# Float64 weights to float32: the integer add of the conversion moves from GpSimd to VectorE

## The chip, the core and the metric

The kernel runs on one core of a Trainium2 chip. The metric is the device time of one launch in microseconds. Before the change it is 1539.69 us, the median of 3 runs (1537.06 to 1542.2); a profile of one execution goes with them.

## What is computed

Attention over queries pooled in pairs, then two MLPs (pairs of dense layers) one behind the other:

```
q_pool = q.reshape(B, H, S // 2, 2, D).mean(axis=3)          # B=4, H=8, S=1152, D=64
scores = (q_pool @ k^T) / sqrt(D);  attn = softmax(scores);  x = attn @ v
x: (2304, 512) tokens
h = x @ w_in;  g = max(0.01 * h, h);              x = g @ w_out      # first MLP, d_ff = 2048
h = x @ w_in2; g = where(h > 0, h, exp(h) - 1);   out = g @ w_out2   # second MLP
```

The weights of both MLPs arrive as float64 (a 128x512 piece is 512 KB), everything else as float32. The products are wanted in nearly full float32 precision: each float32 operand is split into a high part and a low part, and three matmuls (high x high, high x low, low x high) stand for one.

## The kernel before

The work is written down as a list of small operations, each with an engine, a guessed cost, a rank and the buffers that it reads and writes (`Program.add`, L57). `Program.schedule` (L83) plays the list through once with the guessed costs: when an engine is free it takes the ready operation of lowest rank. The start times that come out of it set the order in which instructions are issued, and on the chip each engine then works through its own queue strictly in that order. An operation may issue several instructions; they stand together in the queue.

The attention of four batches (16 pairs of heads) and eight MLP passes (four batches, two layers) overlap: while the attention of one batch runs, the MLP of an earlier batch is worked in between (`PLAN`, L216). TensorE does scores (L452), transposes (L475), attention x v (L496), the first matmul of an MLP (L638) and the second one (L676). VectorE takes row maxima of scores (L457, L459), low parts of the attention weights (L267, `pt`), parts of the activation functions (L651, L659) and sums of partial products (L689). ScalarE does the exponentials (L463) and high parts (L261). GpSimd does the low parts of weights and activations: the line L267 with `wi`, `wo`, `g`, `kn`, `vn`, `qn`.

A weight piece is used in four batches. The first time it comes as float64 and is converted by `convert` (L271), half of it at a time: 128 halves of 128x256 numbers in all. The float32 result is kept in DRAM (L328), and the three later uses load it from there (L323). The conversion of one half is this:

- SyncE loads the half as pairs of 32-bit words into `cr` (L290): `r[:, :, 0]` low words, `r[:, :, 1]` high words. There are two `cr` buffers, so a load waits until the last reader of the half but one is done.
- VectorE shifts the high word left by 3 and masks it (L293), then puts the two top bits back (L296). The result is `ct`.
- ScalarE scales the low word down to the three bits that are still wanted, in place (L299), and takes the magnitude of the high word, read as a float, into `cm` (L301).
- GpSimd adds the three bits to `ct` as an integer (L303).
- VectorE sets values too small to be represented to zero and writes the piece `wr` (L305). ScalarE and GpSimd then split `wr` into `wi` or `wo` (L331 and L333, through `psplit`, L258).

`cr` is free for the next load when L299, L301, L293, L296 and L303 have read it.

Of the kernel before, what the change touches and what calls it, by code (L numbers as in the profile page):

```python
# [9 lines left out]
F32 = mybir.dt.float32  # L10
F32R = mybir.dt.float32r
U32 = mybir.dt.uint32
ACTF = mybir.ActivationFunctionType
ALU = mybir.AluOpType
# [140 lines left out]
def kernel(  # L155
# [20 lines left out]
    V, A, G, PE = nc.vector, nc.scalar, nc.gpsimd, nc.tensor  # L176
# [10 lines left out]
    FT = DFF // 128  # L187
    QSCALE = 0.5 / float(D) ** 0.5
    HB = NQ // 2
    MIN_HI = 2.0 ** (112 - 127) * (1 + 2.0 ** -3)  # L190
    PTB = 4
    CW = 256
    CB = 2
# [47 lines left out]
    prog = Program()  # L241

    def sb(tag, shape, dt=F32, bufs=1):
        return prog.buf(tag, bufs, lambda: sp.tile(shape, dt, tag=tag, name=tag, bufs=bufs))
# [4 lines left out]
    def act(n, accum=False, sbuf=False):  # L249
        return 50 + 0.833 * n + (190 if accum else 0) + (43 if sbuf else 0)  # L250

    def dve(n, fast=False):
        return 66 + (0.52 if fast else 1.05) * n

    def pool(n):
        return 140 + 2.12 * n
# [14 lines left out]
    def convert(rank, dst, src):  # L271

        for n in range(0, 512, CW):
            r = sb("cr", [128, CW, 2], U32, CB)
            t = sb("ct", [128, CW], U32, CB)  # L280
            mag = sb("cm", [128, CW], F32, CB)

            def load(n=n, r=r):
                rv = r.ap.rearrange("p n t -> p (n t)")
                if len(src.shape) == 3:
                    k0, kn = n // src.shape[2], CW // src.shape[2]
                    rv, sv = rv.rearrange("p (c n) -> p c n", c=kn), src[:, k0:k0 + kn, :]
                else:
                    sv = src[:, n:n + CW]
                nc.sync.dma_start(out=rv, in_=sv.bitcast(U32))  # L290

            prog.add("SP", 60, rank - 1, load, w=[r])
            prog.add("DVE", dve(CW, True), rank, lambda r=r, t=t: V.tensor_scalar(  # L293
                out=t.ap, in0=r[:, :, 1], scalar1=3, scalar2=0x3FFFFFF8,
                op0=ALU.logical_shift_left, op1=ALU.bitwise_and), w=[t], r=[(r, 1)])
            prog.add("DVE", dve(CW), rank, lambda r=r, t=t: V.scalar_tensor_tensor(  # L296
                out=t.ap, in0=r[:, :, 1], scalar=0xC0000000, in1=t.ap,
                op0=ALU.bitwise_and, op1=ALU.bitwise_or), w=[t], r=[(r, 1), t])
            prog.add("ACT", act(CW, sbuf=True), rank, lambda r=r: A.activation(  # L299
                out=r[:, :, 0], in_=r[:, :, 0], func=ACTF.Copy, scale=2.0 ** -29), w=[(r, 0)], r=[(r, 0)])  # L300
            prog.add("ACT", act(CW, sbuf=True), rank, lambda r=r, mag=mag: A.activation(  # L301
                out=mag.ap, in_=r[:, :, 1].bitcast(F32), func=ACTF.Abs), w=[mag], r=[(r, 1)])
            prog.add("POOL", pool(CW), rank, lambda t=t, r=r: G.tensor_tensor(  # L303
                out=t.ap, in0=t.ap, in1=r[:, :, 0], op=ALU.add), w=[t], r=[t, (r, 0)])
            prog.add("DVE", dve(CW), rank, lambda n=n, t=t, mag=mag: V.scalar_tensor_tensor(  # L305
                out=dst[:, n:n + CW], in0=mag.ap, scalar=MIN_HI, in1=t.ap.bitcast(F32),
                op0=ALU.is_ge, op1=ALU.mult), w=[(dst, n)], r=[t, mag])

    kept = {}

    def load_w(rank, layer, w_in, w_out, f, mine):

        src = (w_in[:, f * 128:(f + 1) * 128].rearrange("(c p) f -> p c f", p=128),
               w_out[f * 128:(f + 1) * 128, :])
        rs = [mine("wr", [128, 512], F32, WRB, "p", PBUF) for _ in range(2)]
        for i, r in enumerate(rs):
            if w_in.dtype == F32:
                view = (lambda r=r: r.ap.rearrange("p (c n) -> p c n", c=DC)) if i == 0 else lambda r=r: r.ap
                prog.add("SP", 60, rank - 1.5, lambda i=i, view=view: nc.sync.dma_start(
                    out=view(), in_=src[i]), w=[r])  # L320
            elif (layer, f, i) in kept:
                kp = kept[layer, f, i]
                prog.add("SP", 60, rank - 1.5, lambda r=r, kp=kp: nc.sync.dma_start(  # L323
                    out=r.ap, in_=kp.ap), w=[r], r=[kp])
            else:
                convert(rank - CLEAD, r, src[i])
                kp = kept[layer, f, i] = Buf(lambda i=i: dram.tile([128, 512], F32, name=f"w{layer}_{f}_{i}"))
                prog.add("SP", 60, rank, lambda r=r, kp=kp: nc.sync.dma_start(out=kp.ap, in_=r.ap), w=[kp], r=[r])  # L328
        wi = mine("wi", [128, 2, DC, 128], F32R, WIB, "qT", KTB)
        wo = mine("wo", [128, 2, DM], F32R, WOB, "kT", KTB)  # L330
        psplit(rank - 0.5, WH, WL, lambda: wi[:, 0].rearrange("p c n -> p (c n)"),  # L331
               lambda: wi[:, 1].rearrange("p c n -> p (c n)"), lambda: rs[0].ap, 512, (wi, 0), [rs[0]])
        psplit(rank - 0.5, WH, WL, lambda: wo[:, 0], lambda: wo[:, 1], lambda: rs[1].ap, 512, (wo, 0), [rs[1]])  # L333
        return wi, wo
# [3 lines left out]
    for j in range(2):  # L338
        t = sp.tile([128, 2, 128], F32R, name=f"rem{j}")
# [400 lines left out]
    for b, layer, at, wide in PLAN:  # L740
        tags = [(u, size[u]) for u in ("h" * HBUFS + ("t" * TB + "s" * SBUFS if wide else ""))]
        w = ((moe_w_in, moe_w_out), (moe2_w_in, moe2_w_out))[layer]
# [35 lines left out]
```

## Time and profile before

| | |
|---|---|
| median of 3 runs | 1539.69 us |
| span of the profiled execution | 1538.0 us |
| TensorE matmul busy | 1414.5 us (92%) |
| VectorE busy | 1011.8 us (66%) |
| ScalarE busy | 1065.2 us (69%) |
| GpSimd busy | 829.8 us (54%) |
| granted TensorE clock, mean | 0.988 of 2.4 GHz |

The profiled execution's span, first to last instruction, is 1.7 us under the median of the timed runs. Busy shares over the whole span hide that it has stages. Conversions run in two stretches, up to some 80 us and from 200 to 590 us; in the latter VectorE is busy nearly all the time. After 590 us all weights are converted and TensorE is busy nearly all the time.

### The profile page before, as it was taken

The numbers are of one execution on the slowest core, as the hardware profiler recorded it, in microseconds if no ns is written. First come the engines' busy times: TensorE is split into PE (matmuls) and PEld (weight loads), VectorE is DVE, ScalarE is ACT, GpSimd is POOL, SyncE is SP. The second block draws the span as 40 slices with busy tenths as digits, with TensorE's granted clock in tenths as the row PEclk, the third lists the DMA queues.
The fourth block names the chain that finished last, engine by engine and source line by source line (L and its number), as shares of the span: only waits on it lengthen the run. The fifth ranks groups of instructions, "written<-read, shape, count | busy, mean of one in ns | idle before, by whom it ended". The sixth has DMA issues, their size and how long they took to land.

```text
span 1538.0 us, 28928 instructions
## 1 busy us (share of the span) xinstructions
PE 1414.5 (92%) x10288; PEld 1365.5 (89%) x10288; DVE 1011.8 (66%) x2273; ACT 1065.2 (69%) x2901; POOL 829.8 (54%) x840
## 2 busy tenths in 40 slices
PE   5877889988888898999999999999999999999998
PEld 4777788888778887999999999899999998899998
DVE  6999888899998998556665556556665454123222
ACT  6998878776688787676668777676667773443553
POOL 5443355765766667354555555255555445466661
PEclk9999999999999999999999999999999999999999
DMA  4232123344434443222222222222222222323210
GB/s 147 91 115 87 40 77 121 122 130 129 127 119 139 132 143 118 76 75 69 69 68 86 79 78 64 71 71 61 76 71 64 56 63 63 106 77 89 70 55 32
DMA packets 82642, 135.59 MB, mean 88 GB/s; under 512 B 8512, under 2 KB 26944, under 8 KB 82496
## 3 DMA queue, kind: packets, MB, share of 16 engines
q1 hardware_dynamic: 82496, 133.73, 28.5%
q8 instruction: 81, 1.33, 0.4%
q14 instruction: 65, 0.53, 0.1%
HBM read 112.20 MB, written 21.50 MB: 87 GB/s over the span
## 4 chain that ended last, share of the span: by engine, by line
PE 63%; DVE 20%; ACT 7%; DMA 4%; issue 3%; POOL 2%; SPq 0%; ACTq 0%; POOLq 0%; DVEq 0%
PE h L676 16%; PE h L638 16%; PE s L452 8%; PE o L496 7%; PE t L475 5%; DVE m L457 3%; DVE ct L293 3%; DVE wr L305 3%; PE s L638 3%; PE s L676 3%; DVE ct L296 2%; DVE pt L267 2%; PE t L638 2%; PE t L373 2%; PE t L676 2%
## 5 line engine op out<-in xcount | busy, mean ns | idle before, releaser
L676 PE MATMUL h<-g,wo 128*128 128x288 f32 x2460 | 425.8, 303 | 16.7 <-DVE t L659 7.9
L638 PE MATMUL h<-xs,wi 128*128 128x288 f32 x2448 | 418.1, 305 | 23.3 <-DVE t L659 13.5
L638 PEld LDWEIGHTS h<-xs,wi 128*128 128x128 f32 x2448 | 351.8, 190 | 33.1 <-DVE t L659 19.0
L676 PEld LDWEIGHTS h<-g,wo 128*128 128x128 f32 x2460 | 356.9, 189 | 23.1 <-DVE t L659 9.9
L457 DVE TENSOR_REDUCE m<-s 128x1 f32<-128x384 f32 x432 | 231.8, 550 | 71.9 <-PE s L452 68.9
L261 ACT ACTIVATE pt<-t 128x384 fp32r<-128x384 f32 (+2 forms) x426 | 188.0, 456 | 117.3 <-PE t L475 109.1
L463 ACT ACTIVATE p<-s,m 128x384 f32<-128x384 f32 x432 | 249.1, 587 | 19.1 <-DVE m L459 18.7
L267 DVE TENSOR_TENSOR pt<-t,pt 128x384 fp32r<-128x384 f32 (+1 forms) x416 | 206.6, 508 | 74.0 <-ACT pt L261 72.6
L452 PE MATMUL s<-kT,qT 128*128 128x384 f32 x768 | 198.5, 356 | 25.7 <-ACT p L463 25.0
L267 POOL TENSOR_TENSOR g<-t,g 128x288 fp32r<-128x288 f32 x216 | 179.1, 833 | 67.6 <-ACT g L261 62.4
L267 POOL TENSOR_TENSOR wo<-wr,wo 128x512 fp32r<-128x512 f32 x112 | 145.9, 1307 | 108.2 <-ACT wo L261 106.3
L496 PE MATMUL o<-pt,vn 128*128 128x256 f32 (+1 forms) x1152 | 192.1, 302 | 5.4 <-DVE pt L267 3.5
L475 PE MATMUL t<-ident,p 128*128 128x128 f32 x1116 | 181.8, 277 | 12.3 <-DVE pt L267 11.3
L267 POOL TENSOR_TENSOR wi<-wr,wi 128x512 fp32r<-128x512 f32 x110 | 144.0, 1310 | 62.9 <-ACT wi L261 48.9
L496 PEld LDWEIGHTS o<-pt,vn 128*128 128x128 f32 x1152 | 165.1, 190 | 10.4 <-DVE pt L267 10.0
L475 PEld LDWEIGHTS t<-ident,p 128*128 128x128 f32 x1116 | 139.8, 142 | 21.9 <-DVE pt L267 11.8
L452 PEld LDWEIGHTS s<-kT,qT 128*128 128x128 f32 x768 | 126.2, 193 | 32.9 <-ACT p L463 31.8
L303 POOL TENSOR_TENSOR ct<-ct,cr 128x256 uint32<-128x256 uint32 x128 | 98.8, 774 | 95.5 <-DVE ct L296 33.8
L267 POOL TENSOR_TENSOR vn<-raw,vn 128x576 fp32r<-128x576 f32 x32 | 46.3, 1448 | 174.5 <-ACT vn L261 174.5
L261 ACT ACTIVATE g<-t 128x288 fp32r<-128x288 f32 x216 | 95.9, 446 | 44.1 <-DVE t L659 26.2
L689 DVE TENSOR_TENSOR acc<-h,acc 128x288 f32<-128x288 f32 x158 | 71.0, 452 | 66.2 <-PE h L676 64.9
L261 ACT ACTIVATE wo<-wr 128x512 fp32r<-128x512 f32 x112 | 70.5, 630 | 46.3 <-PE h L676 33.5
(150 smaller groups left out, 2228.4 us busy)
## 6 DMA issues: line engine op xcount, KB each, us to landing
wr<-w SPq DMA_DIRECT2D x172, 256.0 KB, 2.7
cr<-in_moe_w_in_dram SPq DMA_DIRECT2D x64, 256.0 KB, 2.8
cr<-in_moe_w_out_dram SPq DMA_DIRECT2D x64, 256.0 KB, 2.7
w<-wr SPq DMA_DIRECT2D x64, 256.0 KB, 2.4
raw<-in_k_dram SPq DMA_DIRECT2D x32, 288.0 KB, 3.0
raw<-in_v_dram SPq DMA_DIRECT2D x32, 288.0 KB, 3.1
raw<-in_q_dram SPq DMA_DIRECT2D x32, 256.0 KB, 2.9
p<-w SPq DMA_DIRECT2D x20, 256.0 KB, 2.6
```

The costliest lines, as they stand in the source:

```text
L261: prog.add("ACT", act(n, sbuf=not psum), rank, lambda: A.activation(out=hi(), in_=src(), func=ACTF.Copy), w=[w], r=r)
L267: lambda: eng.tensor_tensor(out=lo(), in0=src(), in1=f32(hi()), op=ALU.subtract),
L293: prog.add("DVE", dve(CW, True), rank, lambda r=r, t=t: V.tensor_scalar(out=t.ap, in0=r[:, :, 1], scalar1=3, scalar2=0x3FFFFFF8, op0=ALU.l ...
L303: prog.add("POOL", pool(CW), rank, lambda t=t, r=r: G.tensor_tensor(out=t.ap, in0=t.ap, in1=r[:, :, 0], op=ALU.add), w=[t], r=[t, (r, 0)])
L452: PE.matmul(out=st[:, 0:384], lhsT=qa(a), rhs=kT[:, 384 * c:384 * c + 384], start=(i == 0), stop=(i == len(seq) - 1))
L457: prog.add("DVE", dve(384), rank - LR, lambda st=st, c=c: V.tensor_reduce(out=m[:, c:c + 1], in_=st[:, 0:384], axis=AX.X, op=ALU.max), w=[ ...
L463: prog.add("ACT", act(384, True), rank - LE, lambda c=c: A.activation(out=p[:, 384 * c:384 * c + 384], in_=banks[c][:, 0:384], func=ACTF.E ...
L475: PE.transpose(out=t[:, i, :], in_=p[:, (3 * c + i) * 128:(3 * c + i + 1) * 128], identity=ident)
L496: PE.matmul(out=o[:, 0:n], lhsT=vn[:, c, :], rhs=pt[th][:, a, c % 3, :], start=(c == 3 * ORDER[0] and a == 0), stop=(c == 3 * ORDER[2] + 2 ...
L638: PE.matmul(out=h[:, 0:HB], lhsT=wi[:, a, c, :], rhs=xs[c][:, e, cols], start=(c == 0 and a == 0 and e == 0), stop=(c == DC - 1 and a == 1))
L676: PE.matmul(out=y[:, 0:HB], lhsT=w[f][1][:, a, d * 128:(d + 1) * 128], rhs=g[f][:, e, cols], start=(f % FC == 0 and a == 0 and e == 0), st ...
L689: prog.add("DVE", dve(HB), rank - HURRY, lambda y=y, a_=a_, cols=cols: V.tensor_tensor(out=a_[:, cols], in0=y[:, 0:HB], in1=a_[:, cols], o ...
```

## The change

The conversion of a half keeps its load, its two ScalarE instructions and three VectorE instructions, and loses the GpSimd instruction. ScalarE multiplies the high word, read as a float, by 2^-112 (this moves its exponent to where float32 has it; values too small become zero) into `g`, which keeps the tag `cm`. VectorE then shifts `g` left by 3, adds the low word's three bits as integers and puts the sign bit of `g` back, writing the piece. These three are one operation of the schedule, so they stand one behind the other in VectorE's queue, and each reads what the one ahead of it wrote. Lines behind the change have numbers lower by 3 in the changed kernel.

```
-            prog.add("DVE", dve(CW, True), rank, lambda r=r, t=t: V.tensor_scalar(
-                out=t.ap, in0=r[:, :, 1], scalar1=3, scalar2=0x3FFFFFF8,
-                op0=ALU.logical_shift_left, op1=ALU.bitwise_and), w=[t], r=[(r, 1)])
-            prog.add("DVE", dve(CW), rank, lambda r=r, t=t: V.scalar_tensor_tensor(
-                out=t.ap, in0=r[:, :, 1], scalar=0xC0000000, in1=t.ap,
-                op0=ALU.bitwise_and, op1=ALU.bitwise_or), w=[t], r=[(r, 1), t])
+            prog.add("ACT", act(CW, sbuf=True), rank, lambda r=r, g=g: A.activation(
+                out=g.ap, in_=r[:, :, 1].bitcast(F32), func=ACTF.Copy, scale=REBIAS), w=[g], r=[(r, 1)])
             prog.add("ACT", act(CW, sbuf=True), rank, lambda r=r: A.activation(
                 out=r[:, :, 0], in_=r[:, :, 0], func=ACTF.Copy, scale=2.0 ** -29), w=[(r, 0)], r=[(r, 0)])
-            prog.add("ACT", act(CW, sbuf=True), rank, lambda r=r, mag=mag: A.activation(
-                out=mag.ap, in_=r[:, :, 1].bitcast(F32), func=ACTF.Abs), w=[mag], r=[(r, 1)])
-            prog.add("POOL", pool(CW), rank, lambda t=t, r=r: G.tensor_tensor(
-                out=t.ap, in0=t.ap, in1=r[:, :, 0], op=ALU.add), w=[t], r=[t, (r, 0)])
-            prog.add("DVE", dve(CW), rank, lambda n=n, t=t, mag=mag: V.scalar_tensor_tensor(
-                out=dst[:, n:n + CW], in0=mag.ap, scalar=MIN_HI, in1=t.ap.bitcast(F32),
-                op0=ALU.is_ge, op1=ALU.mult), w=[(dst, n)], r=[t, mag])
+            def join(n=n, g=g, t=t, r=r):
+                V.tensor_scalar(out=t.ap, in0=g.ap.bitcast(U32), scalar1=3, scalar2=None, op0=ALU.logical_shift_left)
+                V.tensor_tensor(out=t.ap, in0=t.ap, in1=r[:, :, 0], op=ALU.add)
+                V.scalar_tensor_tensor(
+                    out=dst[:, n:n + CW].bitcast(U32), in0=g.ap.bitcast(U32), scalar=0x80000000, in1=t.ap,
+                    op0=ALU.bitwise_and, op1=ALU.bitwise_or)
+
+            prog.add("DVE", dve(CW, True) + 2 * dve(CW), rank, join, w=[t, (dst, n)], r=[g, (r, 0)])
```

How VectorE's queue changes is seen around one cast of `qn` in the middle of the second stretch. `ct` is the integer result, `wr` the finished piece, `m` a row maximum, `pt` attention weights, `xu` the attention output. Before:

```order
L457 TENSOR_REDUCE m_6430<-s_6412 128x1
L296 SCALAR_TENSOR_TENSOR ct_6417<-cr_6370,ct_6417 128x256
L305 SCALAR_TENSOR_TENSOR wr_6440<-cm_6415,ct_6404 128x256
L509 TENSOR_TENSOR xu_5681<-o_6362,tm_6450 64x320
L305 SCALAR_TENSOR_TENSOR wr_6440<-cm_6433,ct_6417 128x256
L263 CAST qn_6475<-qs_5738 128x512
L457 TENSOR_REDUCE m_6430<-s_6481 128x1
L293 TENSOR_SCALAR ct_6494<-cr_6442 128x256
L296 SCALAR_TENSOR_TENSOR ct_6494<-cr_6442,ct_6494 128x256
L293 TENSOR_SCALAR ct_6510<-cr_6464 128x256
```

The same place of VectorE's queue in the changed kernel, where the shift is L298, the add L299 and the sign L300 (the add is listed as an instruction of its own kind, over 512 elements instead of 256):

```order
L298 TENSOR_SCALAR ct_6519<-cm_6497 128x256
L299 ISA ct_6519<-cr_6448,ct_6519 128x512
L300 SCALAR_TENSOR_TENSOR wr_6474<-cm_6497,ct_6519 128x256
L456 TENSOR_REDUCE m_6458<-m_6458 128x1
L263 CAST qn_6535<-qs_5668 128x512
L298 TENSOR_SCALAR ct_6561<-cm_6545 128x256
L299 ISA ct_6561<-cr_6485,ct_6561 128x512
L300 SCALAR_TENSOR_TENSOR wr_6564<-cm_6545,ct_6561 128x256
L506 TENSOR_TENSOR xu_5815<-o_6414,tm_6566 64x320
```

Before, the three VectorE instructions of a half lie apart, with those of other halves or other work between them; now they are always neighbours, and the second and the third name the `ct` that the one ahead of them writes.

GpSimd's queue around the low part of the same `qn`, before (`ct` is the integer add, the others are low parts):

```order
L267 TENSOR_TENSOR wo_6380<-wr_6356,wo_6380 128x512
L303 TENSOR_TENSOR ct_6404<-ct_6404,cr_6352 128x256
L303 TENSOR_TENSOR ct_6417<-ct_6417,cr_6370 128x256
L267 TENSOR_TENSOR qn_6475<-qs_5738,qn_6475 128x512
L267 TENSOR_TENSOR wi_6479<-wr_6440,wi_6479 128x512
L303 TENSOR_TENSOR ct_6494<-ct_6494,cr_6442 128x256
L303 TENSOR_TENSOR ct_6510<-ct_6510,cr_6464 128x256
```

and in the changed kernel:

```order
L267 TENSOR_TENSOR wo_6523<-wr_6218,wo_6523 128x512
L267 TENSOR_TENSOR qn_6535<-qs_5668,qn_6535 128x512
L267 TENSOR_TENSOR wo_6555<-wr_6376,wo_6555 128x512
L267 TENSOR_TENSOR g_6609<-t1_6580,g_6609 128x288
L267 TENSOR_TENSOR wi_6643<-wr_6298,wi_6643 128x512
```

The 128 adds are gone from GpSimd's queue; all its other work stays. ScalarE keeps its two instructions for a half, now with `cm` ahead of `cr`. The same number of loads and stores is issued by SyncE.

## Rows read from the trace of the kernel before

**Rows 1.** Windows of the whole span: busy us of each engine by stage.
```profile
core 0: us, PE busy (x) PEld busy (x) DVE busy (x) ACT busy (x) POOL busy (x), PEclk, DMA share, GB/s
...
200.00:300.00 100.00, 91.45 (x650) 85.51 (x650) 86.46 (x196) 80.66 (x228) 61.72 (x64) 0.98 0.32 103
300.00:590.00 290.00, 252.06 (x1769) 235.19 (x1767) 276.46 (x580) 220.53 (x619) 188.53 (x200) 0.99 0.42 133
590.00:1538.00 948.00, 917.88 (x6834) 905.83 (x6834) 476.62 (x1083) 594.00 (x1571) 495.98 (x485) 0.99 0.24 71
```

**Rows 2.** Chain that ended last, 300 to 590 us: its shares by line.
```profile
by line: DVE wr L305 10.9%; DVE ct L293 10.6%; DVE ct L296 9.5%; issue 7.9%; DVE m L457 7.2%; DVE pt L267 5.7%; PE h L638 4.8%; DMA cr<-in_moe_w_out_dram 4.6%; DVE acc L689 3.1%; ACT p L463 2.9%; DMA cr<-in_moe_w_in_dram 2.7%; POOL ct L303 
```

**Rows 3.** VectorE's groups by line, whole span: busy, mean ns, idle before.
```profile
L305 DVE SCALAR_TENSOR_TENSOR wr<-cm,ct 128x256 f32<-128x256 f32 x128 | 83.6, 657 | 1.7 <-POOL ct L303 1.6
L296 DVE SCALAR_TENSOR_TENSOR ct<-cr,ct 128x256 uint32<-128x256 uint32 x128 | 80.5, 632 | 0.9
L293 DVE TENSOR_SCALAR ct<-cr 128x256 uint32<-128x256 uint32 x128 | 69.8, 549 | 11.1 <-DMA cr<-in_moe_w_in_dram 8.9 <-DMA cr<-in_moe_w_out_dram 2.1
L538 DVE TENSOR_TENSOR xu<-t,xu 128x512 f32<-128x512 f32 x12 | 8.3, 690 | 0.8 <-PE t L535 0.6
```

**Rows 4.** Tiles ct and qs: durations min/median/max in ns.
```profile
L293 DVE TENSOR_SCALAR ct<-cr x128: 272/294/1524, 7.8 to 587.7; 128x256 uint32<-128x256 uint32 x128
L296 DVE SCALAR_TENSOR_TENSOR ct<-cr,ct x128: 403/425/1659, 9.4 to 589.2; 128x256 uint32<-128x256 uint32 x128
L303 POOL TENSOR_TENSOR ct<-ct,cr x128: 729/747/1034, 11.9 to 589.7; 128x256 uint32<-128x256 uint32 x128
L305 DVE SCALAR_TENSOR_TENSOR wr<-cm,ct x128: 402/416/1678, 12.7 to 591.4; 128x256 f32<-128x256 f32 x128
L399 DVE TENSOR_SCALAR qs<-qs x32: 229/286/1494, 8.6 to 1141.4; 128x256 f32<-128x256 f32 x32
```

**Rows 5.** Timeline of VectorE, 451 to 459 us: start, us, instruction.
```profile
451.92 0.28 DVE L293 TENSOR_SCALAR ct<-cr 128x256 uint32<-128x256 uint32 x1
452.24 0.93 DVE L296 SCALAR_TENSOR_TENSOR ct<-cr,ct 128x256 uint32<-128x256 uint32 x1
453.56 0.54 DVE L457 TENSOR_REDUCE m<-s 128x1 f32<-128x384 f32 x1
454.02 1.68 DVE L305 SCALAR_TENSOR_TENSOR wr<-cm,ct 128x256 f32<-128x256 f32 x1
456.95 1.33 DVE L293 TENSOR_SCALAR ct<-cr 128x256 uint32<-128x256 uint32 x1
458.32 0.42 DVE L296 SCALAR_TENSOR_TENSOR ct<-cr,ct 128x256 uint32<-128x256 uint32 x1
```

**Rows 6.** Timeline of GpSimd in the same stretch.
```profile
452.13 0.75 POOL L303 TENSOR_TENSOR ct<-ct,cr 128x256 uint32<-128x256 uint32 x1 [0.41 <-DVE ct L296]
453.99 1.43 POOL L267 TENSOR_TENSOR vn<-raw,vn 128x576 fp32r<-128x576 f32 x1
456.83 1.30 POOL L267 TENSOR_TENSOR wo<-wr,wo 128x512 fp32r<-128x512 f32 x1 [1.42 <-ACT wo L261]
```

**Rows 7.** GpSimd's groups by line, 300 to 590 us.
```profile
L303 POOL TENSOR_TENSOR ct<-ct,cr 128x256 uint32<-128x256 uint32 x84 | 65.0, 775 | 56.4 <-DVE ct L296 16.7 <-issue 7.1 <-ACT cm L301 4.8
L267 POOL TENSOR_TENSOR g<-t,g 128x288 fp32r<-128x288 f32 x42 | 36.8, 875 | 15.3 <-ACT g L261 12.0 <-DVE ct L293 2.1 <-DVE ct L296 0.9
L267 POOL TENSOR_TENSOR wo<-wr,wo 128x512 fp32r<-128x512 f32 x21 | 28.2, 1343 | 11.4 <-ACT wo L261 10.1 <-DVE ct L293 1.0
L267 POOL TENSOR_TENSOR wi<-wr,wi 128x512 fp32r<-128x512 f32 x21 | 28.2, 1341 | 7.9 <-ACT wi L261 4.7 <-DVE qs L399 1.8 <-PE s L452 1.1
L267 POOL TENSOR_TENSOR kn<-raw,kn 128x576 fp32r<-128x576 f32 x6 | 8.9, 1489 | 2.9 <-ACT kn L261 2.9
```

**Rows 8.** ScalarE's groups by line, 300 to 590 us.
```profile
L299 ACT ACTIVATE cr<-cr 128x256 uint32<-128x256 uint32 x84 | 36.7, 437 | 11.2 <-DMA cr<-in_moe_w_out_dram 8.2 <-DMA cr<-in_moe_w_in_dram 1.4 <-POOL ct L303 0.9
L301 ACT ACTIVATE cm<-cr 128x256 f32<-128x256 f32 x84 | 36.0, 429 | 0.0
```

**Rows 9.** Waits of SyncE's queue, and of TensorE from 300 to 590 us.
```profile
SPq L290 <- POOL ct L303: 188.4, 115, 8.4
PE h L638 <- DVE t L659: 10.3, 11, 1.7
```

More of the change, by code (lines that the diff above doesn't have):

```diff
@@ L189 @@
     HB = NQ // 2
-    MIN_HI = 2.0 ** (112 - 127) * (1 + 2.0 ** -3)
+    REBIAS = 2.0 ** -112
     PTB = 4
@@ L280, in convert @@
             t = sb("ct", [128, CW], U32, CB)
-            mag = sb("cm", [128, CW], F32, CB)
+            g = sb("cm", [128, CW], F32, CB)
             def load(n=n, r=r):
```

## The prediction

> **What bounds the kernel now.** I read the windows by stage first [rows 1]. From 590 us on TensorE is busy 917.9 of 948 us and no weight is converted any more: nothing there can gain or lose by this change but through what is carried into it. From 300 to 590 us it is VectorE that is full, 276.5 of 290 us, which leaves it 13.5 us idle, while TensorE has 37.9 us of idle time. From 200 to 300 us VectorE has 86.5 of 100. The chain of waits says the same of 300 to 590 us [rows 2]: the largest three entries are the three VectorE lines of the conversion, together 31.0%, then other VectorE lines (7.2, 5.7, 3.1%), ahead of TensorE's first entry of 4.8%. GpSimd's add stands below 2.7% there. TensorE's longest wait in that stage is for VectorE [rows 9]. So the change is worth what it does to VectorE's time between 200 and 590 us, and that passes to the end nearly one for one, up to the 37.9 us that TensorE has idle.
>
> Then I looked at why the conversion costs VectorE so much. The three lines have medians of 294, 425 and 416 ns but maxima above 1500 [rows 4] and means of 549, 632 and 657 [rows 3]. The two timelines side by side show what the long ones are [rows 5, 6]: L296 starts at 452.24 while GpSimd's add L303 runs from 452.13 to 452.88, and takes 0.93 us; L293 starts at 456.95, GpSimd runs `wo` from 456.83 to 458.13, and L293 ends at 458.28; L305 starts at 454.02, just behind the start of `vn` (453.99 to 455.42), and takes 1.68 us. A VectorE instruction that reads SBUF alone waits until the GpSimd instruction that is under way is done. Row maxima, which read PSUM, take 0.54 in between. Free of that, the three take their minima, 272 + 403 + 402 = 1077 ns. All of it: busy 83.6 + 80.5 + 69.8 = 233.9 us, free 128 x 1.077 = 137.9, so 96.0 us of VectorE's time is waiting behind GpSimd.
>
> **The change part by part.** All sums are of VectorE's time in the profiled execution, whose span of 1538.0 us lies 1.7 us under the median of 1539.7; I add the result to the median.
>
> ScalarE: two instructions of 437 and 429 ns for a half before [rows 8], two of the same shape after. Nothing. They come first now; VectorE waited for almost none of its conversion inputs before (1.7 and 0.9 us of idle time ahead of L305 and L296, [rows 3]), because it is itself the late one, so I take no new wait for ScalarE. If ScalarE were late, the row maxima and `pt` behind the shift would wait with it.
>
> Instructions on VectorE, free of waiting. The shift L298 is like L293; the nearest row with dense 4-byte operands of 256 is L399, 229 to 286 ns [rows 4]; I take 272, no difference. The sign L300 is like L296: 403. The integer add is not in the trace. Below it is L296, which reads the same strided `cr` and as many bytes: 403 ns. Above it is a two-input operation over 512 elements, since the order lists this add over 512: L538 with 690 ns [rows 3]. I take 490, a third of the way up, nearer to the row that moves the same bytes. Sum 1165 against 1077: +88 ns, x128 = +11 us. Ends: with 229 and 403, -5 us; with 286 and 690, +39 us.
>
> The chain of three. Neighbours that don't depend on each other overlap: L457 ends at 454.10, L305 begins at 454.02. Where the second needs the first, L293 ends at 452.20 and L296 begins at 452.24; at 458.28 and 458.32 again [rows 5]. A dependent neighbour so costs VectorE 0.11 us more. After the change every half has two: 256 x 0.11 = 28.2 us. In the order of before 33 of the 128 L296 stand right behind an L293, 3.6 us. Net +25 us. The Trainium skill ("VectorE: DVE Perf Modes", section "The DRAIN you can't avoid") says otherwise: the next operation can't start until the pipeline of the one ahead is empty in any case, and a semaphore between chained operations costs nothing extra. By that rule this term would be 0; [rows 5] contradict it with 0.04 us of pause against 0.08 us of overlap, and the measurement decides.
>
> Waits behind GpSimd. Adds leave GpSimd, 65.0 of its 188.5 us in the stage [rows 1, 7]. Which share of VectorE's waiting goes with them? A wait found at random lasts in proportion to the length of the one waited for, and so does the chance to meet it: weights are count times mean squared. L303: 84 x 0.775^2 = 50.5. The others: 32.2 (`g`), 37.9 (`wo`), 37.8 (`wi`), 13.3 (`kn`) and, with `vn` and `qn` of about `kn`'s length and count, some 21: together 142. The share is 50.5 / 193 = 26%, of 96.0 us: -25 us. Ends: -15 us if the adds are met less than their share; -44 us by mere count (84 of about 185 instructions).
>
> The rest, 71 us, is waits behind low parts that stay. Three instructions in a block meet a GpSimd instruction less often than three spread out, but in the 0.11 us between two of them GpSimd can start, and then the next one waits for nearly all of its 0.9 to 1.5 us. [Rows 5, 6] have both: L296 behind L293 waits at 452.24 and doesn't at 458.32. I take -10 us, ends 0 and -25.
>
> The freed hop. A load of `cr` waits for L303 115 times [rows 9]; now the add on VectorE frees the buffer, one queue later than the shift, and GpSimd's queue is out of it. GpSimd's add is under 2.7% of the chain in the stage, under 7.8 us; VectorE idles only 0.9 + 1.7 us ahead of L296 and L305, so its own queue takes the place. I count -1 us. Blocks of three hold back row maxima and low parts that TensorE wants by up to a block, 1.4 us and its waits; since VectorE is never without work this moves the order, not the sum: nothing, end +8 us.
>
> Sum: +11 + 25 - 25 - 10 - 1 = 0 us. Predicted 1540 us: what VectorE no longer waits for GpSimd it spends on the longer add and on the pauses of the chain.
>
> **The rivals.**
> A, the forecast, 1540 us, its own range 1529 to 1551, that is a sum of +-11 us.
> B, faster: the blocks rarely meet GpSimd, since its remaining instructions fall between the blocks, and a less busy GpSimd (188.5 - 65.0 = 123.5 of 290 us) is met less. Then some 20 us more of the 71 us go: 1520 us. For it: VectorE's other work between two blocks mostly reads PSUM and lets GpSimd run. Against it: L296 at 452.24, which waited although its neighbour had not.
> C, slower: the integer add works on 512 elements and takes 690 ns. Its place is the middle of every block between 200 and 590 us; the price against my 490 is 128 x 0.2 = 25.6 us: 1566 us. It decides the sign from about 525 ns on (35 ns above my 490, x128 = 4.5 us). For it: the order's 512. Against it: the bytes are those of L296.
> D, the chain costs nothing: the block's instructions follow each other as closely as independent ones do, and without the 25 us the time is 1515 us. The two pauses in [rows 5] speak against it. This is what the Trainium skill's rule named above would make of it.
>
> **How the numbers follow.** A 0.50, B 0.24, C 0.22, D 0.04. About 0.3% (4.6 us) is what a measurement of this kernel can tell from no change. Of A's 0.50, 0.29 lies within 4.6 us of 1539.7, 0.11 below and 0.10 above. Faster 0.11 + 0.24 + 0.04 = 0.39; the same 0.29; slower 0.10 + 0.22 = 0.32. The range takes in the upper part of B's spread past its centre and C nearly to its own, and leaves out about 0.09 of the chance below and 0.10 above: 1516 to 1564 us.
>
> **What would show it.** Windows from 300 to 590 us: GpSimd near 124 us, VectorE still above 270. Groups: the means of shift, add and sign together near 1.64 us over the span (1.165 free and 61 us / 128 of waits; 1.84 before, [rows 3]), with the add's minimum between 0.47 and 0.52 us. Timeline: the add begins 0.03 to 0.04 us behind the shift's end, the sign likewise behind the add. The add's minimum above 0.6 would make C; a mean of the three together under 1.5 us would make B; overlap between shift and add would make D. VectorE waiting for ScalarE's `cm` or `cr` for more than some 10 us in all would show a cost that I left out.

## The result and the profile after

The changed kernel takes 1559.67 us (median of 4 runs, 1556.75 to 1563.19); the kernel before, beside it, 1538.7 (1537.06 to 1542.2). The ratio is 1.0135 [1.0114, 1.0157]: 21 us slower. The forecast, 1540 us, was that nothing would change; 1559.67 lies inside its range of 1516 to 1564, and outside its own case A, which ended at 1551.

The windows of the changed kernel by stage, to be held against [rows 1]:

```profile
core 0: us, PE busy (x) PEld busy (x) DVE busy (x) ACT busy (x) POOL busy (x), PEclk, DMA share, GB/s
200.00:300.00 100.00, 86.68 (x595) 81.56 (x594) 83.26 (x188) 76.29 (x213) 40.32 (x40) 0.95 0.31 100
300.00:590.00 290.00, 243.67 (x1658) 227.45 (x1657) 251.28 (x558) 212.79 (x596) 121.00 (x112) 0.96 0.40 131
590.00:1559.60 969.60, 943.43 (x7046) 930.22 (x7045) 495.70 (x1134) 615.64 (x1630) 505.20 (x492) 0.99 0.23 72
```

The loss is made ahead of 590 us and paid behind it. TensorE is busy 943.4 us after 590 instead of 917.9: it has more left to do, 7046 matmuls instead of 6834. A fifth of that it is behind already at 200 us (996 matmuls done instead of 1038). In the stage itself VectorE is not fuller but emptier, 251.3 us instead of 276.5, so 38.7 us without work instead of 13.5, and TensorE is without work for 46.3 us instead of 37.9. That two engines both wait more is the first thing to explain: it looks like work held up, not like work added. Whom VectorE waits for most from 300 to 590 us, before and after:

```profile
DVE m L457 <- PE s L452: 3.7, 8, 0.9
```

```profile
DVE m L454 <- PE s L449: 11.0, 13, 1.6
```

A row maximum waits for TensorE's scores 11.0 us in all instead of 3.7. So VectorE runs dry where TensorE delivers later, and TensorE in turn waits for VectorE (below).

TensorE's clock is part of the loss too. Its row of the whole span, before and after:

```profile
PE 1414.5 (92%) x10288; PEld 1365.5 (89%) x10288; DVE 1011.8 (66%) x2273; ACT 1065.2 (69%) x2901; POOL 829.8 (54%) x840
```

```profile
PE 1426.4 (91%) x10288; PEld 1376.4 (88%) x10288; DVE 997.5 (64%) x2273; ACT 1068.2 (68%) x2901; POOL 732.1 (47%) x712
```

The same 10288 matmuls keep TensorE busy 11.9 us longer, at a mean granted clock of 0.980 instead of 0.988; the span is 21.6 us longer. In the two stages of the conversion the clock is 0.95 and 0.96 instead of 0.98 and 0.99. One such place: TensorE is busy 13.4 of 20 us, and in the 20 us behind that its clock is 0.86 on the mean, so part of them ran at 1.2 instead of 2.4 GHz.

```profile
440.00:460.00 20.00, 13.39 (x87) 11.35 (x86) 18.28 (x42) 13.75 (x39) 9.38 (x11) 0.97 0.43 134
460.00:480.00 20.00, 18.83 (x116) 17.79 (x116) 15.59 (x37) 14.87 (x45) 6.95 (x7) 0.86 0.35 112
```

No run sets the clock by itself, so it is not shown what the time would be without this.

VectorE's three conversion lines, whole span, as in [rows 3], and then the same lines with minimum, median and maximum, as in [rows 4]:

```profile
L300 DVE SCALAR_TENSOR_TENSOR wr<-cm,ct 128x256 uint32<-128x256 uint32 x128 | 78.8, 616 | 6.3
L299 DVE CUSTOM_DVE_ANT_0 ct<-cr,ct 128x512 uint16<-128x512 uint16 x128 | 76.4, 597 | 13.9 <-ACT cr L295 0.4
L298 DVE TENSOR_SCALAR ct<-cm 128x256 uint32<-128x256 uint32 x128 | 53.9, 421 | 2.0 <-ACT cm L293 1.9
```

```profile
L298 DVE TENSOR_SCALAR ct<-cm x128: 226/284/1533, 8.1 to 595.2; 128x256 uint32<-128x256 uint32 x128
L299 DVE CUSTOM_DVE_ANT_0 ct<-cr,ct x128: 424/426/1582, 8.5 to 595.6; 128x512 uint16<-128x512 uint16 x128
L300 DVE SCALAR_TENSOR_TENSOR wr<-cm,ct x128: 424/426/1547, 9.8 to 596.0; 128x256 uint32<-128x256 uint32 x128
```

The add's median is 426 ns, not 490 and far from 690. The three means make 421 + 597 + 616 = 1634 ns, and free of waiting they are 226 + 424 + 424 = 1074. Idle time ahead of the add is 13.9 us with almost no releaser (0.4): that is the pause.

VectorE's timeline in two blocks, as [rows 5], and below it GpSimd's, as [rows 6]:

```profile
441.34 0.54 DVE L267 TENSOR_TENSOR pt<-t,pt 128x384 fp32r<-128x384 f32 x1
441.81 0.27 DVE L298 TENSOR_SCALAR ct<-cm 128x256 uint32<-128x256 uint32 x1
442.20 0.43 DVE L299 CUSTOM_DVE_ANT_0 ct<-cr,ct 128x512 uint16<-128x512 uint16 x1
442.66 0.42 DVE L300 SCALAR_TENSOR_TENSOR wr<-cm,ct 128x256 uint32<-128x256 uint32 x1
...
444.20 0.28 DVE L298 TENSOR_SCALAR ct<-cm 128x256 uint32<-128x256 uint32 x1
444.61 0.85 DVE L299 CUSTOM_DVE_ANT_0 ct<-cr,ct 128x512 uint16<-128x512 uint16 x1
445.55 0.43 DVE L300 SCALAR_TENSOR_TENSOR wr<-cm,ct 128x256 uint32<-128x256 uint32 x1
```

```profile
444.37 0.81 POOL L267 TENSOR_TENSOR g<-t,g 128x288 fp32r<-128x288 f32 x1 [4.16 <-ACT g L261]
```

In the first block the shift ends at 442.08 and the add begins at 442.20, 0.12 behind it; the sign follows the add at 0.03. Over all 128 blocks the median pauses are 0.123 and 0.035 us, where independent neighbours overlap by 0.08 (`pt` ends at 441.88, the shift begins at 441.81). In the second block GpSimd's low part starts at 444.37, while the shift still runs (444.20 to 444.48), and the add behind the pause takes 0.85. It is so for most: 32 of the 128 adds wait (they last longer than 1.3 times their median), and ahead of 31 of them GpSimd's instruction starts before the shift has ended, 0.19 us before it on the median. The add then ends 0.28 us behind GpSimd's end.

TensorE's longest waits from 200 to 590 us:

```profile
PE t L472 <- DVE pt L267: 9.9, 10, 2.1
PE h L635 <- DVE t L648: 8.8, 5, 3.4
PE h L635 <- DVE t L656: 8.1, 10, 2.8
PE h L673 <- DVE acc L686: 7.5, 6, 2.9
PE o L493 <- DVE pt L267: 5.2, 3, 2.8
```

All of them are waits for VectorE, 39.5 us together. In the kernel before the five longest of the same stretch were waits for VectorE too and made 31.1 us: the 10.3 us in 11 pieces of [rows 9], two of 3.7 and 3.5, and these:

```profile
PE t L475 <- DVE pt L267: 10.1, 13, 2.3
PE t L535 <- DVE rb L525: 3.5, 1, 3.5
```

One single wait was as long there (3.5 us); now four of the five rows have one of 2.8 us or more.

### The profile page after: what moved, and what is told of

Same layout as the page of the kernel before. It is cut to its first block, busy times and chain, and to the rows that moved or that the text cites. A ratio compares the mean times of both kernels' runs of the same rounds, so it can differ in the third digit from the quotient of the medians.

```text
span 1559.6 us, 28777 instructions
## 1 busy us (share of the span) xinstructions
PE 1426.4 (91%) x10288; PEld 1376.4 (88%) x10288; DVE 997.5 (64%) x2273; ACT 1068.2 (68%) x2901; POOL 732.1 (47%) x712
## 4 chain that ended last, share of the span: by engine, by line
PE 55%; DVE 3%; ACT 2%; DMA 1%; issue 1%; POOL 0%; SPq 0%; ACTq 0%; DVEq 0%; POOLq 0%
PE h L673 15%; PE h L635 15%; PE s L449 5%; PE o L493 5%; PE t L472 4%; PE s L635 3%; PE s L673 2%; PE t L635 2%; PE t L673 2%; PE t L370 1%; DVE xs L263 1%; DMA out_dram<-cr 1%; DVE t L656 0%; DVE xs L267 0%; ACT t L651 0%
## 5 line engine op out<-in xcount | busy, mean ns | idle before, releaser
L635 PE MATMUL h<-xs,wi 128*128 128x288 f32 x2448 | 423.1, 308 | 28.4 <-DVE t L656 10.3
L635 PEld LDWEIGHTS h<-xs,wi 128*128 128x128 f32 x2448 | 356.7, 193 | 38.0 <-DVE t L656 15.7
L493 PE MATMUL o<-pt,vn 128*128 128x256 f32 (+1 forms) x1152 | 197.2, 308 | 11.0 <-DVE pt L267 9.0
L493 PEld LDWEIGHTS o<-pt,vn 128*128 128x128 f32 x1152 | 169.9, 195 | 15.4 <-DVE pt L267 14.8
L261 ACT ACTIVATE g<-t 128x288 fp32r<-128x288 f32 x216 | 95.7, 446 | 39.5 <-DVE t L656 22.4
L460 ACT ACTIVATION_READ_ACCUMULATOR p<-s,m 128x1 f32 x432 | 91.7, 212 | 0.0
```

The costliest lines, as they stand in the source:

```text
L261: prog.add("ACT", act(n, sbuf=not psum), rank, lambda: A.activation(out=hi(), in_=src(), func=ACTF.Copy), w=[w], r=r)
L460: prog.add("ACT", act(384, True), rank - LE, lambda c=c: A.activation(out=p[:, 384 * c:384 * c + 384], in_=banks[c][:, 0:384], func=ACTF.E ...
L493: PE.matmul(out=o[:, 0:n], lhsT=vn[:, c, :], rhs=pt[th][:, a, c % 3, :], start=(c == 3 * ORDER[0] and a == 0), stop=(c == 3 * ORDER[2] + 2 ...
L635: PE.matmul(out=h[:, 0:HB], lhsT=wi[:, a, c, :], rhs=xs[c][:, e, cols], start=(c == 0 and a == 0 and e == 0), stop=(c == DC - 1 and a == 1))
```

## The experiments

Three theories were tested. First theory: the block itself, three instructions that each read what the one ahead wrote, costs by its pauses and by what it holds back. Second: the new order that the scheduler makes of the change. Third: the add on VectorE, which GpSimd did before. Each experiment is told by its edit against the changed kernel, unless it says otherwise. The edits are shortened: "..." marks what is left out, and functions stand under short names. A time is the median of 4 runs (7 for e2_block_old), and each ratio is to the kernel before, measured beside it.

**The block taken apart (e1_split).** The three instructions are scheduled each by itself; 34 dependent neighbours are left of 256.

```
-            prog.add("DVE", dve(CW, True) + 2 * dve(CW), rank, join, w=[t, (dst, n)], r=[g, (r, 0)])
+            prog.add("DVE", dve(CW, True), rank, shift, w=[t], r=[g])
+            prog.add("DVE", dve(CW), rank, add, w=[t], r=[t, (r, 0)])
+            prog.add("DVE", dve(CW), rank, sign, w=[(dst, n)], r=[g, t])
```

> The same three VectorE instructions of a half as in the changed kernel, but each an operation of its own, so that the schedule can put other work between them (34 dependent neighbours instead of 256). Theory 1 (the block: pauses between dependent neighbours, overlap lost, and TensorE's suppliers held back behind three instructions): about 0.3 us x 220 / 2 = 34 us of VectorE's time come back, 1525 to 1540 us, ratio to before 0.99 to 1.00. Theory 2 (the other order of loads and attention that the new costs give): little changes, 1550 to 1565 us. Theory 3 (VectorE now does the add that GpSimd did): little changes too, 1550 to 1565 us.

1513.42 us, ratio 0.983 [0.9806, 0.9855]: faster than before by 26 us, and faster than any theory had forecast, with the same arithmetic on the same engines as the changed kernel. The third theory falls as the cause.

**The add on GpSimd, the rest apart (e4_gp_add).** The edit is against e1_split.

```
-            prog.add("DVE", dve(CW), rank, add, w=[t], r=[t, (r, 0)])
+            prog.add("POOL", pool(CW), rank, lambda t=t, r=r: G.tensor_tensor(
+                out=t.ap, in0=t.ap, in1=r[:, :, 0], op=ALU.add), w=[t], r=[t, (r, 0)])
```

> ScalarE rebases as in the changed kernel; shift and sign on VectorE and the add on GpSimd, each an operation of its own: VectorE has two instructions for a half instead of three. Theory 3 (VectorE's extra work costs the time): clearly faster than the split with the add on VectorE, by some 128 x 0.34 = 44 us of VectorE's time less 25 us of waits behind the adds: 1515 to 1530 us. Theory 1 (the block): faster than the changed kernel by 20 us or more, and near the split. Theory 2 (new order): 1550 us or more.

1503.44 us, 0.9764 [0.974, 0.9789]. With the add on GpSimd it takes 10 us less than with it on VectorE, where the three instructions stand apart in both. So the add's place is worth something, about a fifth of the 46 us that lie between e1_split and the changed kernel.

**The block in the old order (e2_block_old).** The instructions of TensorE, ScalarE and SyncE stand as in the kernel before, and the block of three stands where L305 stood; the load buffers are four instead of two, and the rebased word and the sum stay in the load's and the result's own buffers, so that it has room. The edit is against the kernel before; the removed instructions keep empty places in the schedule.

```
-            prog.add("POOL", pool(CW), rank, ..., w=[t], r=[t, (r, 0)])
-            prog.add("DVE", dve(CW), rank, ..., w=[(dst, n)], r=[t, mag])
+            prog.add("DVE", dve(CW), rank, lambda: (shift(), add(), sign()), w=[(dst, n)], r=[t, g])
```

> The order of before on TensorE, ScalarE and SyncE to the letter; the conversion's three VectorE instructions stand as one block where L305 stood, shift and add work in place in the finished piece, the rebased word stays in its load buffer, of which there are four instead of two (the memory of ct and cm pays for them). Theory 1 (the block): still slow, 1550 us or more. Theory 2 (the new order): near before, 1532 to 1545 us. Theory 3 (add on VectorE): 1550 us or more as well. The two more load buffers can only help.

1547.37 us, 1.0058 [1.0037, 1.0079]: slower than before in before's own order, and e1_split is fast in a new one. The second theory falls as the whole cause. It does not fall as a part: the expectation gave 1550 us or more to the block and 1545 or less to the order, and the time lies between. The 12 us from here to the changed kernel can be the order, the two load buffers more or the longer pauses there, and no run takes these apart. Its lines:

```profile
L308 DVE CUSTOM_DVE_ANT_0 wr<-cr,wr 128x512 uint16<-128x512 uint16 x128 | 73.1, 571 | 4.4
L311 DVE SCALAR_TENSOR_TENSOR wr<-cr,wr 128x256 uint32<-128x256 uint32 x128 | 72.0, 562 | 4.4
```

The idle time ahead of the add is 4.4 us here, that is 128 x 0.034, where the changed kernel had 13.9. By the programs, the add waits for one semaphore here, the one that tells that the shift is done (VectorE's own). In the changed kernel 104 of the 128 adds wait for three (the load's, ScalarE's and VectorE's), and there a separate instruction ahead of the add, which does nothing but wait, has VectorE's.

**Two halves interleaved (e6_pairs).** One operation of six: both shifts, both adds, both signs, so that no instruction stands right behind the one it reads. One line of the scheduler keeps it from waiting for itself.

```
+        def join():
+            for n, r, t, g in half: V.tensor_scalar(... logical_shift_left)
+            for n, r, t, g in half: V.tensor_tensor(... add)
+            for n, r, t, g in half: V.scalar_tensor_tensor(... sign)
```

> The two halves of a piece as one operation of six VectorE instructions: both shifts, both adds, both signs. No neighbour depends on the one ahead of it, but the block is twice as long. Theory 1a (it is the pauses that cost): 20 us faster than the changed kernel or more, 1525 to 1540 us. Theory 1b (it is the holding back of other work behind the block): no faster than the changed kernel, 1555 to 1580 us. Theory 2 (new order): cannot be told from this one.

1520.85 us, 0.9873 [0.9845, 0.9901]: 39 us below the changed kernel, though the block is twice as long, and 4 us below its forecast.

**The same six as three operations of two (e9_twos).** The edit is against e6_pairs.

```
-        prog.add("DVE", 2 * dve(CW, True) + 4 * dve(CW), rank, join, ...)
+        prog.add("DVE", 2 * dve(CW, True), rank, shifts, w=ts, r=gs)
+        prog.add("DVE", 2 * dve(CW), rank, adds, w=ts, r=ts + [(r, 0) for r in rs])
+        prog.add("DVE", 2 * dve(CW), rank, signs, w=[(dst, n) for n, _, _, _ in half], r=gs + ts)
```

> The six instructions of a piece as three operations of two: both shifts, both adds, both signs; other work can go between. No pauses, as in the block of six, which ran in 1521 us, but nothing is held behind more than two. If holding back is what makes the six slower than the split (1513 us) though it waits 20 us less behind GpSimd, this is at the split or below it, 1503 to 1515 us. If not, it stays near 1520 us.

1500.87 us, 0.9765 [0.9743, 0.9787], another 20 us (17 by the ratios), and 2 us below its forecast. The edit changes how long other work is held back; where that work goes instead, the order, follows from it. The stage of 300 to 590 us, e6_pairs first and e9_twos below:

```profile
300.00:590.00 290.00, 266.93 (x1921) 256.15 (x1919) 245.13 (x620) 237.91 (x675) 135.20 (x130) 0.98 0.42 137
```

```profile
300.00:590.00 290.00, 267.61 (x1959) 258.59 (x1958) 259.32 (x629) 241.42 (x680) 143.02 (x138) 0.99 0.42 138
```

TensorE gets through 1921 and 1959 matmuls where the changed kernel had 1658, and is without work for 23.1 and 22.4 us instead of 46.3. Between the two, then, TensorE's idle time in this stage hardly differs. Most of the difference is busy time, for as many matmuls, over the whole span:

```profile
PE 1411.1 (93%) x10288; PEld 1370.8 (90%) x10288; DVE 956.5 (63%) x2273; ACT 1064.0 (70%) x2901; POOL 728.6 (48%) x712
```

```profile
PE 1396.9 (93%) x10288; PEld 1358.5 (91%) x10288; DVE 964.3 (64%) x2273; ACT 1062.5 (71%) x2901; POOL 728.7 (49%) x712
```

That is 14.2 of the 23.5 us between the profiled executions, at a mean granted clock of 0.984 in e6_pairs and 0.993 in e9_twos.

**Blocks of three without dependent neighbours (e11_threes).** This is the direct test of the first theory: a block as long as the change's, holding shift, shift, add, and then add, sign, sign.

```
+        def first(): shift(t0, g0); shift(t1, g1); add(t0, r0)
+        def second(): add(t1, r1); sign(n0, t0, g0); sign(n1, t1, g1)
+        prog.add("DVE", 2 * dve(CW, True) + dve(CW), rank, first, w=[t0, t1], r=[g0, g1, (r0, 0)])
+        prog.add("DVE", 3 * dve(CW), rank, second, w=[(dst, n0), (dst, n1), t1], r=[g0, g1, t0, t1, (r1, 0)])
```

> The six VectorE instructions of two halves as two operations of three, ordered so that no instruction stands right behind the one whose result it reads: shift, shift, add; and add, sign, sign. Blocks as long as the change's, without its 256 dependent neighbours; everything else as in the version with three operations of two (1500.9 us) and the one with a single operation of six (1520.9 us). If the pauses of dependent neighbours are what makes the change slow, and holding back grows with the length of a block, this lies between those two: 1510 us (range 1500 to 1522), with the neighbours in a block overlapping by some 0.08 us. If a block of three by itself, whatever it holds, is what makes the change slow, it stays at 1545 us or more.

1511.12 us, 0.9824 [0.9807, 0.984]: on the forecast, and 48.6 us below the changed kernel at the same block length. Its groups, and its tiles:

```profile
L309 DVE SCALAR_TENSOR_TENSOR wr<-cm,ct 128x256 uint32<-128x256 uint32 x128 | 65.0, 547 | 0.0
L306 DVE CUSTOM_DVE_ANT_0 ct<-cr,ct 128x512 uint16<-128x512 uint16 x128 | 60.3, 481 | 0.2 <-DVE ct L303 0.2
L303 DVE TENSOR_SCALAR ct<-cm 128x256 uint32<-128x256 uint32 x128 | 45.4, 387 | 8.6 <-ACT cm L295 8.2
```

```profile
L303 DVE TENSOR_SCALAR ct<-cm x128: 233/287/1516, 8.2 to 574.2; 128x256 uint32<-128x256 uint32 x128
L306 DVE CUSTOM_DVE_ANT_0 ct<-cr,ct x128: 402/417/1678, 9.7 to 575.0; 128x512 uint16<-128x512 uint16 x128
L309 DVE SCALAR_TENSOR_TENSOR wr<-cm,ct x128: 405/417/1662, 10.5 to 576.3; 128x256 uint32<-128x256 uint32 x128
```

The idle time ahead of the add is 0.2 us instead of 13.9, ahead of the sign 0.0 instead of 6.3. And the instructions themselves are shorter: the means make 1415 ns instead of 1634 (busy times leave out overlap, so means are compared). Over the minima that is (1415 - 1040) x 128 = 48.0 us of waiting, against (1634 - 1074) x 128 = 71.7 in the changed kernel. It is above all the adds and signs that wait less: 13 of the adds and 19 of the signs last longer than 1.3 times their median, where in the changed kernel 32 and 34 do; of the shifts 27 do, against 32. The timeline of e11_threes shows an add that begins 0.08 us ahead of the end of the shift before it (444.62), which belongs to the other half:

```profile
444.33 0.29 DVE L303 TENSOR_SCALAR ct<-cm 128x256 uint32<-128x256 uint32 x1 [0.69 <-ACT cm L295]
444.54 0.42 DVE L306 CUSTOM_DVE_ANT_0 ct<-cr,ct 128x512 uint16<-128x512 uint16 x1
```

**ScalarE's low word first (e7_low_first).** The add then waits for two semaphores, since ScalarE's has been waited for by the shift; the wait for VectorE's moves into the add itself.

```
-            prog.add("ACT", ..., lambda r=r, g=g: A.activation(out=g.ap, ... scale=REBIAS), w=[g], r=[(r, 1)])
             prog.add("ACT", ..., lambda r=r: A.activation(out=r[:, :, 0], ... scale=2.0 ** -29), w=[(r, 0)], r=[(r, 0)])
+            prog.add("ACT", ..., lambda r=r, g=g: A.activation(out=g.ap, ... scale=REBIAS), w=[g], r=[(r, 1)])
```

> The changed kernel with ScalarE's two instructions of a half in the other order, low word first, so that the add waits for two semaphores instead of three (the shift, which waits for the rebase, has already waited for the low word). If the pause ahead of the add grows with the number of semaphores (0.123 us with three in the changed kernel, 0.034 us with one in the block with before's order), it is near 0.08 us here, and the time falls by 128 x 0.045 = 6 us, to about 1554 us. If the pause belongs to the kind of instruction, it stays 0.12 us and the time 1560 us.

1556.87 us, 1.014 [1.0113, 1.0167], no measurable gain over the change's 1.0135. The expectation missed: the pause did not fall in proportion, it fell all the way to 0.034 us. What decides is not the number of semaphores but where the wait for the first instruction stands. In the changed kernel 13 signs wait for two and pause 0.104 us, with VectorE's in the separate instruction ahead; 24 adds and 18 signs there have VectorE's wait in themselves beside a separate one, as all adds have here, and pause 0.034. The add and the shift in groups:

```profile
L299 DVE CUSTOM_DVE_ANT_0 ct<-cr,ct 128x512 uint16<-128x512 uint16 x128 | 78.1, 610 | 4.4
L298 DVE TENSOR_SCALAR ct<-cm 128x256 uint32<-128x256 uint32 x128 | 54.1, 423 | 5.3 <-ACT cm L295 5.1
```

So 13.9 - 4.4 = 9.5 us of pauses went, and the time did not follow. Two rows on why, of the same kernel:

```profile
441.33 0.28 DVE L298 TENSOR_SCALAR ct<-cm 128x256 uint32<-128x256 uint32 x1
441.64 0.94 DVE L299 CUSTOM_DVE_ANT_0 ct<-cr,ct 128x512 uint16<-128x512 uint16 x1
```

The add begins 0.03 behind the shift, but GpSimd's `g` had started at 441.50, and the add takes 0.94 instead of 0.85: where GpSimd is in, a shorter pause only makes a longer wait. 31 adds wait, before it was 32. That takes back at most 31 x 0.09 = 2.8 of the 9.5 us, and VectorE waits 5.1 us for ScalarE's `cm` instead of 1.9, another 3.2. The remaining 3.5 us are under the half width of the interval (4 us). So this run doesn't show what a pause costs at the end.

**One dependent pair more in the kernel before (e8_before_pair).** L293 and L296 as one operation, nothing else changed. That is 101 dependent neighbours more and not 95: of the 33 that stood together before, 27 have the pause in the trace; the other 6 overlap by 0.08 us, their L293 is that of another half. The edit is against the kernel before.

```
-            prog.add("DVE", dve(CW, True), rank, shift, w=[t], r=[(r, 1)])
-            prog.add("DVE", dve(CW), rank, top_bits, w=[t], r=[(r, 1), t])
+            prog.add("DVE", dve(CW, True) + dve(CW), rank, top, w=[t], r=[(r, 1)])
```

> The kernel before with L293 and L296 of a half as one operation, so that they are always neighbours and the second depends on the first; nothing else changes. If a dependent neighbour costs VectorE 0.11 us that pass to the end, 95 more of them cost 10 us: 1546 to 1554 us, ratio 1.005 to 1.01. If pauses are hidden because VectorE has idle time elsewhere, or if it was the move of the add that cost the changed kernel its time, the ratio is 1.000.

1551.34 us, 1.0084 [1.0057, 1.0111]: 13 us, where 101 x 0.11 us is 11. The cost is there in the old kernel too, from a block of two, without the add on VectorE and without ScalarE's new work.

**Twos with the adds on GpSimd (e10_gp_twos).** The edit is against e9_twos.

```
-        prog.add("DVE", 2 * dve(CW), rank, adds, w=ts, r=ts + [(r, 0) for r in rs])
+        for n, r, t, g in half:
+            prog.add("POOL", pool(CW), rank, lambda r=r, t=t: G.tensor_tensor(... add), w=[t], r=[t, (r, 0)])
```

> As the last one with the adds on GpSimd, each an operation of its own: two shifts together, two signs together. It looks for a version below the 1503 us of the split with the add on GpSimd. If VectorE's time still decides, fewer waits behind GpSimd give 1495 to 1503 us; if TensorE is the bound by now or the pairing holds up the loads, 1503 to 1512 us.

1507.74 us, 0.981 [0.979, 0.983]: not better than e9_twos. Its sign and its shift:

```profile
L308 DVE SCALAR_TENSOR_TENSOR wr<-cm,ct 128x256 uint32<-128x256 uint32 x128 | 82.6, 685 | 1.1 <-POOL ct L314 1.1
L304 DVE TENSOR_SCALAR ct<-cm 128x256 uint32<-128x256 uint32 x128 | 56.5, 473 | 11.0 <-ACT cm L295 10.6
```

The adds took 57.4 us of VectorE in e9_twos (488 ns on the mean). Of that, 24 us come back as waits of the sign, 685 ns on the mean beside GpSimd's adds against 496 (128 x 0.189), and VectorE waits 10.6 us for ScalarE's `cm` instead of 3.8. What takes the rest was not traced.

The fastest are e9_twos (0.9765 [0.9743, 0.9787]) and e4_gp_add (0.9764 [0.974, 0.9789]), both 2.4% below the kernel before and 3.7% below the change; the measurement doesn't tell them apart.

## Why the prediction was right or wrong

The time lies in the forecast's range, but by luck: the range reached so far up for rival C, an add of 690 ns, which didn't come. The sum forecast no change, and 21 us were measured. Its terms one by one:

- **What bounds.** Right in the main: VectorE from 200 to 590 us decides, and TensorE pays from 590 us on (25.5 us more busy). That TensorE's clock would move with it (0.988 to 0.980) was in no term.
- **ScalarE at nothing.** Right: VectorE waited 1.9 + 0.4 us for it.
- **Instructions, +11.** Too dear. 1074 ns free of waiting against 1077: 0 us. The add was taken at 490 and is 424 to 426. Rival C (690 ns, 1566 us) is near the measured time and yet wrong: its own sign, an add above 0.6, is not there.
- **The chain of three, +25.** Too cheap. The sign's median pause is the 0.035 of [rows 5], but the add's is 0.123, which no row of before had, for a separate instruction waits for the shift there. With the lost overlap of 0.08 each: 128 x (0.123 + 0.035 + 0.16) = 40.7 us of VectorE's time, less 27 x 0.11 = 3 that were there before: +38. By the rule that the prediction drew from the Trainium skill ("VectorE: DVE Perf Modes", section "The DRAIN you can't avoid"), a semaphore between chained operations costs nothing extra, and the term would be 0; the section adds, which the prediction left out, that a next operation that isn't held starts earlier. The runs disagree with the 0: the pauses are 13.9 + 6.3 us of idle time, and e11_threes, the same instructions with other neighbours, is 48.6 us faster than the change. Rival D falls with it.
- **Waits behind GpSimd, -25 and -10.** By means over minima they go from (657 + 632 + 549 - 1077) x 128 = 97.4 to 71.7 us: -26 in all. The adds' part is as forecast; the -10 for meeting GpSimd less often in a block was not there. The prediction named a reason itself ("in the 0.11 us between two of them GpSimd can start") and weighed it too low: without pauses a block of three has 48.0 us. But its picture of that reason isn't in the rows. The pause is 0.04 us, 0.11 is its cost; and GpSimd's L303 starts at 452.13 [rows 6], while the shift runs until 452.20 [rows 5]. What the traces show is the count: in the changed kernel 98 of 384 conversion instructions wait, in e11_threes, whose neighbours overlap, 59. Why closing up keeps GpSimd away is not shown. (One bound was off: by mere count the share is 84 of the 200 instructions of [rows 1], not of 185, which makes its end -40 and not -44.)
- **The freed hop, -1.** Nothing at VectorE shows against it: it stood idle 2.0 us ahead of the shift. SyncE's waits for a free `cr` grew, though: from 200 to 590 us 269.6 us behind the add, before 156.4 behind L303 and 53.3 behind L301.
- **Blocks hold back row maxima and low parts: nothing, end +8.** Here the forecast failed in kind. "Since VectorE is never without work this moves the order, not the sum" took a full VectorE for granted. Held back, TensorE and ScalarE deliver later, and VectorE itself runs dry: in the stage it has 38.7 us without work, of which the pauses of 85 blocks are 85 x 0.158 = 13.4, and the rest, 25.3, is more than the 13.5 of before; 11.0 of it are row maxima that wait for TensorE's scores. That a long block costs is shown by e6_pairs against e9_twos, 17 to 20 us for six in a piece instead of two. That it costs by holding back is argued from these waits; the order and TensorE's clock change with it.

The terms as they came out: 0 + 38 - 26 - 1 = +11 us, and 21 were measured. The other 10 are put to holding back by difference; no run measures them by themselves at this block length, and the new order, which e2_block_old leaves room for, and the lower clock are in them. The sum also takes a us of VectorE's time as a us at the end, which e7_low_first, with 9.5 us of pauses less and no gain, doesn't confirm. Against the forecast's sum: the add 11 less, the chain 13 more, the waits 9 more, the rest 10 more, together +21.

Of what was named as a sign: GpSimd in the stage 121.0 us (near 124: right); the three means together 1.634 (1.64: right, yet from a shorter add and longer waits); the add's minimum 0.424 (0.47 to 0.52: wrong); VectorE above 270 (251.3: wrong, the row that gave the failed step away); the add 0.03 to 0.04 behind the shift (0.12: wrong), the sign so behind the add (right).

## What to carry to other kernels

On a full VectorE, don't put an instruction right behind the one whose result it reads: a second, independent strand interleaved with it took 48.6 us out of 1560 here, with the same instructions. Keep what is issued as one piece short, two rather than six. An engine that others feed can run dry when it keeps them waiting, however full its row looks. When a forecast nets out to zero from large terms of both signs, the terms are what has to be measured.

## What the runs showed of the hardware

- The pause between dependent VectorE neighbours is 0.034 us where the second one itself waits for the first one's semaphore (all in e2_block_old; the adds in e7_low_first). In the changed kernel it is 0.123 (104 adds), 0.104 (13 signs) and 0.091 (18 signs) where that wait stands in a separate instruction ahead of the second. Independent neighbours overlap by 0.08.
- A pause of 0.034 us lets about as many adds wait behind GpSimd as one of 0.123: 31 of 128 (e7_low_first) and 32 (the changed kernel); where neighbours overlap 13 do (e11_threes). In the changed kernel, by the records, GpSimd starts while the shift ahead of such an add still runs, 0.19 us before its end on the median.
- The 32-bit integer add of two tensors, listed over 512 elements of 16 bits, has a minimum of 402 to 424 ns and a median of 416 to 426 for 256 words, as long as the two-input operation on 256 words beside it.
